# Masks carried as rows of the score products, attention moved earlier, and four more pairs by seven products, in a fused sparse-attention and bilinear-FFN kernel

## The chip, the cores and the metric

The kernel runs on one core of one Trainium2 chip. A core has a matrix engine (PE, with its weight loads shown apart as PEld), three engines for elementwise work (DVE, ACT and POOL), an engine that mostly issues transfers (SP), and 16 DMA engines. Each engine works through its own queue in order and waits on semaphores. The metric is device microseconds (us) of one execution. Three executions of the kernel before took 326.38, 330.83 and 331.78 us, a median of 330.83 us.

## The reference

Eight batches of eight heads, 576 tokens, head size 64. Heads 0 to 3 attend to the last 32 tokens, heads 4 to 7 to earlier tokens of the same residue modulo 32. The attention's output, 4608 rows of 512, goes through a bilinear FFN.

```python
scores = scale * np.matmul(q, k.transpose(0, 1, 3, 2))          # (8, 8, 576, 576)
rel = pos[:, None] - pos[None, :]
mask_local = (rel >= 0) & (rel < 32)                            # heads 0..3
mask_strided = (rel >= 0) & (pos[None, :] % 32 == pos[:, None] % 32)   # heads 4..7
scores = np.where(mask, scores, -1e9)
attn = softmax(scores)                                          # then attn @ v
x = attn_out.transpose(0, 2, 1, 3).reshape(4608, 512)
out = ((x @ w_a) * (x @ w_b)) @ w_out                           # 512 -> 1536 -> 512
```

## The kernel before, in words

**Tiles and slots.** The FFN runs over nine tiles `t` of 512 tokens. A tile has 16 slots: slots 0 to 11 make `x @ w_a` and `x @ w_b` for one block of 128 of the 1536 columns each (`ffn_ab`, block `f`), slots 12 to 15 make the output (`ffn_ys`, from tile 1 on). In a common slot PE makes eight matmuls of 512 columns into two PSUM banks, ACT copies the `w_a` bank to `a_sb` (L638), and DVE multiplies it with the `w_b` bank into `pf` (L641, L643). In tile 0 the banks come from a pool of three (`mm`); later a fourth (`tp`) joins the rotation (`mm_bank`).

**Seven products.** A pair `g` of blocks (slots 2g and 2g+1) can make its `x @ w_a` part by seven half-size products instead of eight (`a_pair_mid`, L676, in tiles 3 to 6, and `a_pair`, L736, in tiles 7 and 8). It sums into the banks X, Y and Z, copies X out several times with ACT (L714 to L731), and X's next product waits for each copy. Its inputs are differences of x quarters made by DVE (`xsum_make`, L672). `MID_A` and `FAST_A` name the pairs. The output is made in the same way: `y_plan` (L871) makes 14 groups of six matmuls of 256 columns in `Y_ORDER`, two groups for each of the products 1, 7, 6, 4, 5, 2, 3; after the second, `y_post` (L845) copies the bank with ACT (1, 7, 6, 5, 3) or adds it with DVE (4, 2).

**Attention between the slots.** Batch `b` is one of eight; its steps stand in the tables `STEPS`, `LATER` and `IN_Y` under a slot, and each is put behind that slot's work (or, at a half, between the two products of the following slot; under "y", behind that many of the 14 groups). A unit `u` is half of two heads: u = 0 to 3 are local, 4 to 7 strided. `S` makes scores into the one `st` bank pair (L381) and takes their exponent with ACT (L401), then DVE clears masked elements of `p` with a bitwise AND (`S_m`, L419). `V` multiplies by v: for local units through the `o` bank, a reciprocal and a product by DVE (L462, L470, L488); for strided units from the third batch on by `step_VT` (L510): four matmuls into `o`, four into `e` (one bank each from tile 3 on, L521), logarithms and an exponential by ACT (L533, L534), and two products by DVE (L536) that free `o` and `e`. `O` and `I` carry local outputs through DRAM to `xT`, the FFN's input.

**How q and k come.** From the third batch on, POOL issues the loads to DRAM scratch, SP issues transposing DMAs (`step_D`) into `kT_buf[b % 2]` and `qT`, and DVE copies each head of a pair to its own half of the rows of `qz_buf[b % 2]` (`step_Q`, L338); the other half is zero, so that one matmul makes the scores of both heads side by side (192 columns for local, 144 for strided units).

**POOL.** It issues the loads of q, k, v and all weights, and each issue can wait for an earlier transfer (semaphores in a ring of eight). Functions that are registered under a slot (`do(i, ...)`) stand in their engine's queue behind everything of the earlier slots. A tiny POOL copy (`pace`, L1134) holds POOL back to the work of its slot from slot 14 on; before that, nothing but its own waits does. `fill_v` (L112), under slot 0, stands behind the loads of the first two batches and of `w_a` and `w_b`, ahead of those of `w_out`.

Of the kernel before, what the change touches and what calls it, by code (L numbers as in the profile page):

```python
# [8 lines left out]
BF16 = mybir.dt.bfloat16  # L9
# [15 lines left out]
VW = 128  # L25
WCH = (0, 2, 5, 9, 12)
FAST_Y = (1, 2, 3, 4, 5, 6, 7, 8)
MID_A = {t: (1, 3) for t in (3, 4, 5, 6)}
FAST_A = {7: (1, 2, 3, 4, 5), 8: (0, 1, 2, 3, 4, 5)}
# [3 lines left out]
def kernel(  # L33
# [34 lines left out]
    def open_psum(stack, **bufs):  # L68
        for nm, n in bufs.items():
# [13 lines left out]
    kT_buf = [(const.tile([128, 2, PAD + S], BF16, name=f"kT{i}l"), const.tile([128, 2, RS * GP + 48], BF16, name=f"kT{i}s"))  # L83
              for i in range(2)]
    vl_buf = [const.tile([128, HL * 6, VW], BF16, name=f"vl{i}") for i in range(2)]
# [10 lines left out]
    def select(t, op, base, pattern, cm):  # L96
        nc.gpsimd.affine_select(out=t, in_=t, compare_op=op, fill=0.0, base=base, pattern=pattern,
                                channel_multiplier=cm)
# [1069 lines left out]
```

## Time and profile before

| | us |
|---|---|
| median of three executions | 330.83 |
| lowest, highest | 326.38, 331.78 |
| the profiled execution | 323.88 |
| its span, first to last instruction | 322.2 |
| PE busy in it | 313.8 (97%) |
| DVE busy | 248.4 (77%) |
| ACT busy | 191.4 (59%) |
| POOL busy | 120.2 (37%) |

The profile describes one execution. A line of a group gives source line, engine, operation, names out<-in, shapes and count, then the busy time of the group, the mean duration of one in ns, and the idle time of the engine before them. A line of the timeline gives the start and the duration in us, and in brackets how long the engine was idle before and who ended that. Matmuls are pipelined: the duration of one is its latency, and the distance of two starts is what it costs.

### The profile page before, as it was taken

What the parts mean: (1) busy time and instruction counts of PE and PEld (TensorE: products, weight loads), DVE (VectorE), ACT (ScalarE), POOL (GpSimd) and SP (SyncE); (2) the same over time, 40 slices, a digit from 0 to 9 for tenths busy, and PEclk for the clock granted to TensorE, in tenths of its full rate; (3) what the DMA queues carried; (4) which work ended last, traced back from release to release, by engine and by line L of the source; (5) the groups of instructions that cost most, each with busy time, mean ns of one, the idle gap of its engine ahead of it and who ended that gap; (6) DMA issues with size and microseconds to landing.
All of it is one profiled execution on the core that took longest, in us unless ns stands there. A gap on an engine that the chain in (4) does not pass through costs nothing. (4 is left out here: it accounts for less than half of the span.)

```text
span 322.2 us, 7287 instructions
## 1 busy us (share of the span) xinstructions
PE 313.8 (97%) x2738; PEld 217.9 (68%) x2766; DVE 248.4 (77%) x569; ACT 191.4 (59%) x371; POOL 120.2 (37%) x211
## 2 busy tenths in 40 slices
PE   8999999999999999999999999999999999999994
PEld 7764555455775578556999996559655866786684
DVE  6665797488867988899689868997799667857862
ACT  6763767355854476557655766577656655535541
POOL 8844850881255344315340435134001003203520
PEclk9999999999999999999999999999999999999999
DMA  8999999999599999999997999999235040004004
GB/s 154 146 203 199 203 190 209 174 146 152 119 126 144 209 148 104 144 157 172 123 120 151 164 108 131 158 203 135 18 85 121 2 127 5 0 4 130 3 0 130
DMA packets 127811, 40.41 MB, mean 125 GB/s; under 512 B 115616, under 2 KB 124896, under 8 KB 127584
## 3 DMA queue, kind: packets, MB, share of 16 engines
q0 software_dynamic: 80400, 19.28, 65.3%
q1 hardware_dynamic: 47232, 20.61, 35.9%
q8 instruction: 21, 0.34, 0.5%
q14 instruction: 14, 0.11, 0.1%
q10 hardware_dynamic: 144, 0.07, 0.1%
HBM read 39.12 MB, written 18.28 MB: 178 GB/s over the span
## 5 line engine op out<-in xcount | busy, mean ns | idle before, releaser
L617 PE MATMUL mm<-xT,wb_sb 128*128 128x512 bf16 (+1 forms) x301 | 71.6, 357 | 0.4
L617 PE MATMUL mm<-xT,wa_sb 128*128 128x512 bf16 (+1 forms) x287 | 70.2, 356 | 0.6
L638 ACT COPY a_sb<-mm 128x512 f32<-128x512 f32 x68 | 39.7, 584 | 29.5 <-PE mm L617 27.8
L1134 POOL CAST pace<-pf 1x1 f32<-1x1 bf16 x68 | 18.5, 273 | 87.6 <-DVE pf L641 41.0
L617 PEld LDWEIGHTS <-wb_sb 128*128 128x128 bf16 x312 | 30.0, 98 | 27.8 <-issue 0.7
L641 DVE TENSOR_TENSOR pf<-a_sb,mm 128x512 bf16<-128x512 f32 x58 | 39.4, 680 | 9.4 <-ACT a_sb L638 5.7
L401 ACT ACTIVATE p<-st 72x576 bf16<-72x576 f32 (+1 forms) x56 | 36.4, 650 | 15.4 <-PE st L381 14.7
L617 PEld LDWEIGHTS <-wa_sb 128*128 128x128 bf16 x312 | 27.9, 98 | 17.8
L886 PEld LDWEIGHTS <-ps 128*128 128x128 bf16 x336 | 32.6, 98 | 4.1 <-issue 0.5
L886 PE MATMUL mm<-wf,ps 128*128 128x256 bf16 x252 | 30.0, 273 | 0.3 <-ACT y_sb L851 0.3
L851 ACT COPY y_sb<-mm 128x512 f32<-128x512 f32 (+1 forms) x32 | 17.9, 558 | 19.1 <-PE mm L886 16.4
L1134 POOL COPY pace<-y_sb 1x1 f32<-1x1 f32 x21 | 8.4, 401 | 51.2 <-DVE y_sb L849 23.6
L886 PEld LDWEIGHTS <-pf 128*128 128x128 bf16 x252 | 23.6, 98 | 2.7
L766 PE MATMUL mm<-xT,wb_sb 128*128 128x512 bf16 x83 | 25.3, 379 | 0.1
L241 POOL DMA_DIRECT2D vs<-in_v_dram x24 | 21.7, 905 | 4.1 <-issue 1.7
L886 PE MATMUL mm<-wo_sb,pf 128*128 128x256 bf16 x168 | 21.8, 273 | 0.0
L820 DVE TENSOR_TENSOR ps<-pf 128x512 bf16<-128x512 bf16 (+1 forms) x49 | 19.6, 399 | 0.8
L702 PE MATMUL mm<-xT,wb_sb 128*128 128x512 bf16 (+1 forms) x80 | 19.1, 337 | 0.0
L419 DVE TENSOR_TENSOR p<-p,mask_l 128x576 int16<-128x576 int16 x32 | 14.5, 452 | 5.6 <-ACT p L401 5.5
L536 DVE TENSOR_TENSOR xT<-o,xr 64x288 bf16<-64x288 f32 x16 | 7.6, 477 | 13.5 <-ACT xr L534 13.4
L462 PEld LDWEIGHTS <-p 128*128 128x128 bf16 (+1 forms) x256 | 12.9, 97 | 7.1 <-DVE xl L488 1.1
L488 DVE TENSOR_TENSOR xl<-o,rc 96x384 bf16<-96x384 f32 x24 | 13.3, 553 | 0.8
(212 smaller groups left out, 644.0 us busy)
## 6 DMA issues: line engine op xcount, KB each, us to landing
out_dram<-y_sb SPq DMA_DIRECT2D x14, 512.0 KB, 4.6
kr<-in_k_dram POOLq DMA_DIRECT2D x12, 288.0 KB, 6.2
qr<-in_q_dram POOLq DMA_DIRECT2D x12, 288.0 KB, 7.1
vl<-in_v_dram POOLq DMA_DIRECT2D x6, 384.0 KB, 9.3
out_dram<-y_sb SPq DMA_DIRECT2D x7, 256.0 KB, 5.5
vs<-in_v_dram POOLq DMA_DIRECT2D x24, 72.0 KB, 4.9
xd<-xl SPq DMA_DIRECT2D x12, 144.0 KB, 3.3
wo_sb<-in_moe_w_out_dram POOLq DMA_DIRECT2D x4, 384.0 KB, 10.7
```

Source lines behind the costliest of these rows:

```text
L241: nc.gpsimd.dma_start(out=vs_buf[b % 2][:, h, :, 0:D], in_=v[b, HL + h].rearrange("(p r) d -> p r d", r=RS))
L401: nc.scalar.activation(p_flat(p)[:M, :2 * W].rearrange("p (i n) -> p i n", n=2 * n), st[:M].rearrange("p a (i n) -> p (a i) n", n=256)[:, ...
L419: nc.vector.tensor_tensor(pi, pi, mk, op=ALU.bitwise_and)
L617: nc.tensor.matmul(ps_[:, c0:c0 + n], lhsT=w[:, kk, 128 * f:128 * (f + 1)], rhs=xT[:, kk, x0:x0 + n], start=(kk == first and c0 == 0), sto ...
L638: nc.scalar.copy(a_sb, ab[0])
L641: nc.vector.tensor_mul(pf[:, f, :].rearrange("p (i a s) -> p a i s", i=2, s=16), halves(a_sb), halves(ab[1]))
L702: nc.tensor.matmul(dst, lhsT=wb_sb[:, kk, 128 * f:128 * (f + 1)], rhs=rhs, start=kk == 0 and k in (None, 0), stop=kk == KD - 1 and k in (N ...
L766: nc.tensor.matmul(got[e], lhsT=wb_sb[:, kk, 128 * f:128 * (f + 1)], rhs=xT[:, kk, x0:x0 + TTOK], start=kk == 0, stop=kk == KD - 1)
L820: nc.vector.tensor_tensor(s[:, n], a, b, op=op)
L851: nc.scalar.copy({"1": part(0, 0), "7": part(0, 1), "6": part(1, 0), "5": part(1, 1)}[k], bank)
L886: nc.tensor.matmul(bank[b][:, q], lhsT=lhs(g, q), rhs=rhs(g), start=k in "172" and q == 0 and g == 0, stop=g == FG - 1, skip_group_check=True)
L1134: nc.gpsimd.tensor_copy(pace, done)
```

## The change

- **Masks as rows.** From the third batch on the half of the rows that was zero carries a code of the mask, in both `kz` (two buffers for k, one per head of a pair) and `qz_buf[0]`, so that a masked element's score comes out far below zero and its exponent is 0. The AND (`S_m`) goes from there. Each head gets its own matmul: two of 96 or 72 columns in place of one of 192 or 144.
- **New copies.** `step_K` copies each head's rows from `kT_buf[0]` to `kz[j]`, two local and two strided copies of 64x1152 for each batch: by DVE, but by ACT for the local ones (K0, K1) from batch 5 on. `kz` and `qz_buf[0]` are now the same for all batches.
- **Codes.** `code_make`, on POOL behind `fill_v` under slot 0, makes four small tables by ten instructions (four MEMSETs, six selects). `fill_code` copies them into the rows: on DVE under slots 1 to 4 and 14, on ACT under slots 2, 3, 4, 5, 12 and 14 (one copy of 1152 to 1216 elements each). POOL's clearing of `qz_buf[0]` under slots 14 and 15 goes.
- **Positions.** New tables `THIRD`, `FOURTH` and `LATER`. For batches 5 to 7 S0, S1 and V0 stand within the output slots of two tiles before, the local V, O and I are earlier, V4 and V5 stand at 5.5 and 9.5; for batches 4 to 7 S7, V6 and V7 stand behind groups 1, 2 and 5 of the output (before: 2, 6 and 11), and the x differences for the next tile behind groups 7 to 10. The strided `step_D` moves from slots 10 and 11 to 8.
- **Pairs.** Tiles 4 to 6 make pairs 0, 2, 4 by seven products (before 1, 3), tile 3 pairs 2, 4, and tile 7 also pair 0. In `a_pair_mid` one matmul group of `w_b` moves ahead and pair 0 swaps two banks.

```diff
 VW = 128
+BIG = 4096.0
 WCH = (0, 2, 5, 9, 12)
 FAST_Y = (1, 2, 3, 4, 5, 6, 7, 8)
-MID_A = {t: (1, 3) for t in (3, 4, 5, 6)}
-FAST_A = {7: (1, 2, 3, 4, 5), 8: (0, 1, 2, 3, 4, 5)}
+MID_A = {3: (2, 4), 4: (0, 2, 4), 5: (0, 2, 4), 6: (0, 2, 4)}
+FAST_A = {7: (0, 1, 2, 3, 4, 5), 8: (0, 1, 2, 3, 4, 5)}
...
     qT = (const.tile([128, 2, S], BF16, name="qTl"), const.tile([128, HL * W], BF16, name="qTs"))
-    kT_buf = [(const.tile([128, 2, PAD + S], BF16, name=f"kT{i}l"), const.tile([128, 2, RS * GP + 48], BF16, name=f"kT{i}s"))
-              for i in range(2)]
-    vl_buf = [const.tile([128, HL * 6, VW], BF16, name=f"vl{i}") for i in range(2)]
+    kT_three = [(const.tile([128, 2, PAD + S], BF16, name=f"kT{i}l"), const.tile([128, 2, RS * GP + 48], BF16, name=f"kT{i}s"))
+                for i in range(3)]
+    kT_buf, kz = kT_three[::2], kT_three[1:]
+    vl_buf = [const.tile([128, HL * 6, D + 2], BF16, name=f"vl{i}") for i in range(2)]
...
         select(msl, ALU.is_ge, -1, [[-1, LW]], 1)
+    code = const.tile([32, 5, 32], BF16, name="code")
+    minus, even, odd, near = (code[:, i] for i in range(4))
+    eye = ident[:32, :32]
+    def code_make():
+        nc.gpsimd.memset(minus, -1.0)
+        nc.gpsimd.memset(even, -BIG)
+        nc.gpsimd.memset(odd, BIG)
+        nc.gpsimd.memset(near, -BIG)
+        select(minus, ALU.is_equal, 0, [[1, 32]], -1)
+        for t, op, base, step, cm, fill in ((even, ALU.is_ge, 0, 1, -1, BIG), (odd, ALU.is_ge, 0, 1, -1, -BIG),
+                                            (near, ALU.is_ge, 0, -1, 1, -4 * BIG), (near, ALU.is_ge, 1, 1, -1, -4 * BIG),
+                                            (near, ALU.is_ge, -1, 0, 1, -4 * BIG)):
+            select(t, op, base, [[step, 32]], cm, fill)
+    def kz0_zero():
+        nc.vector.memset(kT_three[1][0][:, :, :PAD], 0.0)
+        nc.vector.memset(kT_flat(kT_three[1][1])[:, HL * W:], 0.0)
+    def fill_code(nm, j, part):
+        r = 64 * (1 - j)
+        wide = lambda t, n: t.unsqueeze(1).unsqueeze(1).to_broadcast([32, 2, n, 32])
+        if part < 3:
+            t = kz[j][0] if nm == "k" else qz_buf[0][j][0]
+            t = t.rearrange("p c (g t) -> p c g t", t=32)
+            n = t.shape[2]
+            if part == 2:
+                src = (eye if nm == "k" else near)[:, :n].unsqueeze(1).unsqueeze(3).to_broadcast([32, 2, n, 32])
+                nc.scalar.copy(t[r + 32:r + 64], src)
+            else:
+                src = ((eye, minus) if nm == "k" else (even, odd))[part]
+                nc.vector.tensor_copy(t[r:r + 32, :, part::2], wide(src, (n + 1 - part) // 2))
+        elif nm == "k":
+            t = kz[j][1].rearrange("p c n -> p (c n)")[r:r + 64, :HL * W].rearrange("p (h i c) -> p h i c", h=HL, c=4)
+            nc.scalar.copy(t, nm_l[:64, :NP].unsqueeze(1).unsqueeze(3).to_broadcast(list(t.shape)))
+        else:
+            t = qz_pair[0][1][r:r + 64, j].rearrange("p c g n -> p (c g) n")
+            nc.vector.tensor_copy(t, nm_r[:64].unsqueeze(1).to_broadcast(list(t.shape)))
...
         r = slice(64 * j, 64 * j + 64)
-        dst = qz_buf[b % 2][j][z][r]
+        dst = qz_buf[0][j][z][r]
         nc.vector.tensor_copy(dst.rearrange("d c r n -> d (c r n)") if z else dst, qT[z][r])
+    def step_K(b, z, j):
+        r = slice(64 * j, 64 * j + 64)
+        part = (lambda t: kT_flat(t)[r, :HL * W]) if z else (lambda t: t[r, :, PAD:])
+        (nc.vector.tensor_copy if z or b < FIRST_D + 3 else nc.scalar.copy)(part(kz[j][z]), part(kT_buf[0][z]))
...
         kT = kT_buf[b % 2][c // 2]
         st = pst.tile([128, 2, 512], F32, tag="st", name="st")
...
                 k0 = (G * half + i) * (LW if c < 2 else GP)
-                if c < 2:
-                    rhs = qz_pair[b % 2][0][:, c % 2, :, k0:k0 + n]
-                elif b < FIRST_D:
-                    rhs = qz_pair[b % 2][1][:, :, c % 2, G * half + i]
-                if c < 2 or b < FIRST_D:
-                    lhs = kT[:, c % 2, k0:k0 + 128]
-                else:
-                    k0 = W * (u - HL) + i
-                    lhs = kT_strided(b)[:, k0:k0 + 509:4]
-                    rhs = qz_pair[b % 2][1].rearrange("p j c (e h) n -> p j (c e) h n", h=HL)[:, :, i, u - HL]
-                nc.tensor.matmul(sv[:, i, :2 * n].rearrange("p (j n) -> p j n", j=2), lhsT=lhs, rhs=rhs, start=True, stop=True)
+                if b < FIRST_D:
+                    rhs = qz_pair[1][0][:, c % 2, :, k0:k0 + n] if c < 2 else qz_pair[1][1][:, :, c % 2, G * half + i]
+                    nc.tensor.matmul(sv[:, i, :2 * n].rearrange("p (j n) -> p j n", j=2), lhsT=kT[:, c % 2, k0:k0 + 128],
+                                     rhs=rhs, start=True, stop=True)
+                    continue
+                for j in range(2):
+                    if c < 2:
+                        lhs, rhs = kz[j][0][:, c % 2, k0:k0 + 128], qz_buf[0][j][0][:, c % 2, k0:k0 + n]
+                    else:
+                        k0 = W * (u - HL) + i
+                        lhs = kT_flat(kz[j][1])[:, k0:k0 + 509:4]
+                        rhs = qz_pair[0][1][:, j].rearrange("p c (e h) n -> p (c e) h n", h=HL)[:, i, u - HL]
+                    nc.tensor.matmul(sv[:, i, j * n:(j + 1) * n], lhsT=lhs, rhs=rhs, start=True, stop=True)
             return
...
         S_px(b, u)
-        S_m(b, u)
+        if b < FIRST_D:
+            S_m(b, u)
...
                  12.6: "S1", 12.75: "L0 X2", 13: "s2 X3 V0 m2 L1 W3", 13.5: "V1 S3", 14: "V2 X0", 14.5: "V3", 15: "X1"},
-             2: {18: "Q0 Q1", 20: "S0", 20.5: "S1", 21: "V0", 21.5: "S2 Q2", 22: "V1 Q3", 22.5: "S3 O0", 23: "V2", 23.5: "S4",
+             2: {18: "K0 K1 Q0 Q1", 20: "S0", 20.5: "S1", 21: "V0 K2", 21.5: "S2 Q2", 22: "V1 K3 Q3", 22.5: "S3 O0", 23: "V2", 23.5: "S4",
                  24: "V3 I0 O1", 24.5: "S5", 25.5: "V4", 26: "S6", 26.5: "I1", 27: "V5", 27.5: "S7", 28.5: "V6", 30: "V7"}}
-    LATER = {-4: "Q0", -3: "Q1", -1: "S0", 0: "S1", 1: "V0", 2: "S2 Q2", 3: "V1 O0", 4: "S3 I0 Q3", 5: "V2", 6: "S4", 7: "V3 O1", 8: "S5", 9: "V4 I1",
-             10: "S6",
-             11: "V5"}
-    IN_Y = {2: "S7", 6: "V6", 11: "V7"}
+    THIRD = {-4: "K0 Q0", -3: "K1 Q1", -1: "S0", 0: "S1", 1: "V0 K2", 2: "S2 Q2", 3: "V1 K3 O0", 4: "S3 I0 Q3", 5: "V2", 6: "S4", 7: "V3 O1",
+             8: "S5", 9: "V4 I1", 10: "S6", 11: "V5", ("y", 2): "S7", ("y", 6): "V6", ("y", 11): "V7"}
+    REST = {4: "V3 O1 S4", 5.5: "V4", 7: "I1", 8: "S5", 9.5: "V5", 11: "S6", ("y", 1): "S7", ("y", 2): "V6", ("y", 5): "V7",
+            ("y", 7): "x0", ("y", 9): "x1 x2", ("y", 10): "x3"}
+    FOURTH = {-4: "K0 Q0", -3: "K1 Q1", -1: "S0", 0: "S1 K2", 1: "V0 S2 Q2", 2: "V1 O0 S3 K3", 3: "V2 I0 Q3", **REST}
+    LATER = {-7: "K0", -6: "K1 Q0", -5: "Q1", ("y", -6): "S0", -3: "K2", ("y", -3): "S1", ("y", -2): "V0", -2: "K3",
+             0: "S2 Q2", 1: "V1 O0", 2: "S3 Q3", 2.5: "V2", 3: "I0", **REST}
     FN = {"Tk": step_Tk, "Tq": step_Tq, "S": step_S, "V": step_V, "X": step_X, "W": lambda b, n: fast_w(n, slice(0, 3)),
           "s": S_px, "m": S_m, "L": lead_vl, "O": rows_out, "I": rows_in, "Pk": lambda b, c: pair_up("k", c), "Pq": lambda b, c: pair_up("q", c),
-          "Q": lambda b, n: step_Q(b, n // 2, n % 2)}
+          "Q": lambda b, n: step_Q(b, n // 2, n % 2), "K": lambda b, n: step_K(b, n // 2, n % 2),
+          "x": lambda b, n: xsum_make(b, n)}
...
         Y, Z, b1, b0 = [mm_bank([128, TTOK]) for _ in range(4)]
+        if g == 0:
+            Z, b1 = b1, Z
         Y, Z = Y[:, :HT], Z[:, :HT]
...
         yield p7[:1, :1]
+        b_mm(b0, 0, (0,))
         P(X, ws(0), xs(0))
         nc.scalar.copy(quarter(1, 1), X)
-        b_mm(b0, 0, (0,))
+        b_mm(b0, 0, (1,))
         P(Z, w(1, 1), xs(3))
...
         add(quarter(1, 1), p7)
-        b_mm(b0, 0, (1, 2, 3))
+        b_mm(b0, 0, (2, 3))
         P(X, ws(3), x(1, 1))
...
         do(0, fill_v, vs_buf[0])
+        do(0, code_make)
+        do(2, kz0_zero)
         for c in range(4):
...
                 do(g0 + (12 if b == FIRST_D + 1 else 7), load_vl, b)
-            gs = {2: (13, 14, 15, 15), 3: (6, 6, 14, 15)}.get(b) or (3, 4, 10, 11)
+            gs = {2: (13, 14, 15, 15), 3: (6, 6, 14, 15)}.get(b) or (3, 4, 8, 8)
             for (z, nm), g in zip(((0, "k"), (0, "q"), (1, "k"), (1, "q")), gs):
...
                 do(16 * 2 + (2, 5, 7, 9, 11, 13, 14, 15)[2 * n + c], wsum_make, n, c)
-        for t in MID_A:
-            do(16 * t - 1, xsum_make, t, 0)
-            for n in (1, 2, 3):
-                do(16 * t, xsum_make, t, n)
-        do(16 * (NT - 2) - 1, xsum_make, NT - 2, 0)
-        for n in (2, 1, 3):
-            do(16 * (NT - 2), xsum_make, NT - 2, n)
+        do(47, xsum_make, 3, 0)
+        for n in (1, 2, 3):
+            do(48, xsum_make, 3, n)
         for n in range(4):
...
         do(4, zero_qz, 1, nc.vector, ((1, 0),))
-        for i, jz in ((14, (0, 0)), (14, (1, 0)), (15, (0, 1)), (15, (1, 1))):
-            do(i, zero_qz, 0, nc.gpsimd, (jz,))
+        do(1, fill_code, "q", 0, 3)
+        do(1, fill_code, "q", 1, 3)
+        for i, j in ((2, 0), (3, 1)):
+            for part in (2, 0, 1):
+                do(i, fill_code, "q", j, part)
+        do(4, fill_code, "k", 0, 3)
+        for part in (0, 1):
+            do(4, fill_code, "k", 0, part)
+        do(5, fill_code, "k", 0, 2)
+        do(12, fill_code, "k", 1, 3)
+        for part in (2, 0, 1):
+            do(14, fill_code, "k", 1, part)
         do(2, fill_v, vs_buf[1])
```

More of the change, by code (lines that the diff above doesn't have):

```diff
@@ L94, with select @@
     msl = const.tile([128, LW], F32, name="msl")
-    def select(t, op, base, pattern, cm):
-        nc.gpsimd.affine_select(out=t, in_=t, compare_op=op, fill=0.0, base=base, pattern=pattern,
+    def select(t, op, base, pattern, cm, fill=0.0):
+        nc.gpsimd.affine_select(out=t, in_=t, compare_op=op, fill=fill, base=base, pattern=pattern,
                                 channel_multiplier=cm)
@@ L314, in T_e, with kT_flat @@
                     perm(qz_buf[b % 2][j][c // 2][pr, c % 2]), tv[pr])
-    def kT_strided(b):
-        return kT_buf[b % 2][1].rearrange("p c n -> p (c n)")
+    def kT_flat(t):
+        return t.rearrange("p c n -> p (c n)")
     def step_D(b, z, nm):
@@ L324, in step_D @@
         if z == 0:
-            nc.sync.dma_start(out=kT_buf[b % 2][0][:, :, PAD:] if nm == "k" else qT[0],
+            nc.sync.dma_start(out=kT_buf[0][0][:, :, PAD:] if nm == "k" else qT[0],
                               in_=rows.rearrange("t h d -> t (h d)"), transpose=True)
         elif nm == "k":
-            nc.sync.dma_start(out=kT_strided(b)[:, :HL * W], in_=rows.rearrange("h (t e) d -> (h t) (e d)", e=2), transpose=True)
+            nc.sync.dma_start(out=kT_flat(kT_buf[0][1])[:, :HL * W], in_=rows.rearrange("h (t e) d -> (h t) (e d)", e=2), transpose=True)
         else:
@@ L1056 @@
         for b in range(1, B):
-            for pos, names in (STEPS.get(b) or {16 * (b - 1) + x: n for x, n in LATER.items()}).items():
+            for pos, names in (STEPS.get(b) or (THIRD if b == 3 else FOURTH if b == 4 else LATER)).items():
+                if isinstance(pos, tuple):
+                    pos = ("y", b - 1, pos[1]) if pos[1] > 0 else ("y", b - 2, 14 + pos[1])
+                elif b not in STEPS:
+                    pos += 16 * (b - 1)
                 steps.setdefault(pos, []).append((b, names.split()))
-            if b not in STEPS:
-                for n, names in IN_Y.items():
-                    steps["y", b - 1, n] = [(b, names.split())]
         at = {}
```

## The prediction

> **What bounds the kernel now.** I read the engines' shares first, then the groups with shapes kept apart, then the timelines around the waits that the change makes or moves. The first line of the page:
>
> ```profile
> PE 313.8 (97%) x2738; PEld 217.9 (68%) x2766; DVE 248.4 (77%) x569; ACT 191.4 (59%) x371; POOL 120.2 (37%) x211
> ```
>
> PE is busy throughout; from 22 us on the chain of waits hardly leaves it. So a time is won only by fewer columns on PE, and lost whenever an engine makes PE wait. Groups of PE (mean duration of one behind the comma):
>
> ```profile
> L617 PE MATMUL mm<-xT,wb_sb 128*128 128x512 bf16 x237 | 62.9, 379 | 0.4
> ...
> L462 PE MATMUL o<-vl,p 128*128 128x65 bf16 x192 | 11.0, 194 | 0.8 <-DMA vl<-in_v_dram 0.5 <-DVE xl L488 0.3
> ...
> L521 PE MATMUL o<-p,vs 72*128 72x72 bf16 x128 | 8.1, 196 | 0.0
> L381 PE MATMUL st<-qz1s,kT1s 128*128 128x144 bf16 x64 | 6.6, 226 | 0.0
> L381 PE MATMUL st<-qz1l,kT1l 128*128 128x192 bf16 x48 | 6.6, 246 | 0.0
> ```
>
> These durations are latencies. In the timeline four 72-column products together take 0.29, so one costs (0.29 - 0.196) / 3 = 0.03 us; in the same way 96 columns cost 0.043 (the transposes), 144 0.061, 192 0.082, 256 0.109, 512 0.216.
>
> Next POOL's timeline, where the new tables will be made:
>
> ```profile
> 22.21 0.68 POOL L236 DMA_DIRECT2D tk<-in_v_dram  x1 [2.72 <-PE ab L617]
> ...
> 28.77 0.76 POOL L250 DMA_DIRECT2D wb_sb<-in_moe_w_b_dram  x1 [1.98 <-DMA wb_sb<-in_moe_w_b_dram]
> ...
> 31.78 1.80 POOL L112 MEMSET vs<- 72x2016 bf16 x1
> 33.50 3.02 POOL L253 DMA_DIRECT2D wo_sb<-in_moe_w_out_dram  x4
> ```
>
> The MEMSET is `fill_v`, registered under slot 0, which PE leaves at about 22.4. POOL is 9 us late because its issues wait for earlier transfers (8.1 us of idle in this stretch). ACT at that time is at slot 2:
>
> ```profile
> 23.98 0.58 ACT L638 COPY a_sb<-mm 128x512 f32<-128x512 f32 x1 [0.32 <-PE mm L617]
> 25.66 0.59 ACT L638 COPY a_sb<-mm 128x512 f32<-128x512 f32 x1 [1.10 <-PE mm L617]
> ```
>
> Last, an output phase (groups of 12 matmuls), where V6 and V7 move closer:
>
> ```profile
> 220.97 0.29 PE L521 MATMUL o<-p,vs 72*128 72x72 bf16 x4
> ...
> 221.22 0.58 ACT L851 COPY y_sb<-mm 128x512 f32<-128x512 f32 x1 [0.77 <-PE mm L886]
> ...
> 221.83 0.43 ACT L533 ACTIVATE xr<-o 64x288 f32<-64x288 f32 x1
> ...
> 222.60 0.68 ACT L534 ACTIVATE xr<-xr 64x576 f32<-64x576 f32 x1
> 223.32 0.47 DVE L536 TENSOR_TENSOR xT<-o,xr 64x288 bf16<-64x288 f32 x1 [2.02 <-ACT xr L534]
> 223.70 0.46 DVE L536 TENSOR_TENSOR xT<-e,xr 64x288 bf16<-64x288 f32 x1
> ...
> 224.51 0.30 PE L521 MATMUL o<-p,vs 72*128 72x72 bf16 x4
> ```
>
> V6 begins at 220.97, behind group 6; `o` is free 2.82 us later, `e` 3.19 us later; V7 begins 3.54 us later, behind group 11. It has 0.7 us to spare.
>
> **The parts.**
>
> *Columns.* A local unit goes from 3 x 0.082 = 0.246 to 6 x 0.043 = 0.258, a strided one from 4 x 0.061 = 0.244 to 8 x 0.033 = 0.264: with 48 units +0.6 to +0.8 us. Four more pairs go from 8 x 0.216 = 1.73 to 14 x 0.109 = 1.53: -0.8. Net about **-0.2**. No row shows weights taken with a step of four for 72 columns; those weight loads last 113 ns against 98 in a row, so the price of 192 of them lies between 0 and 192 x 0.015 = +2.9. I take 0, since 72-column products with fresh weights run at 0.03 (L521).
>
> *The wait for the tables.* In the changed kernel's order ACT has, right behind slot 2's copy (23.98 to 24.57), the copy of `near`, which waits for POOL's last select. POOL makes the tables behind `fill_v`: 33.6 plus four MEMSETs of some 0.11 and six selects of 0.28 to 0.36 (rows of L97) gives 36.0. Then ACT takes 1.15 for its copy of 1152 elements (row L122: 64x1152, 1149 ns) and 0.58 for slot 3's `a_sb`: 37.7. Behind the waiting ACT stand all later `a_sb` copies. DVE waits too, behind slot 2's multiply. With three banks PE gets through slot 3 and the first half of slot 4; slot 4's `w_b` matmuls need slot 3's `w_a` bank, which ACT has not copied. They began at 27.19. PE has nothing else in its queue: **37.7 - 27.2 = +10.5** (9 to 11.5, as the transfers land). Nothing wins it back, since PE is full afterwards. POOL's `w_out` loads go 2.4 us later, but before PE needs them; ACT's other code copies lie in its idle time (in slots 2 to 5 a copy of 0.58 each 1.73; under slots 12 and 14 idle stretches of 0.6 and 2.1).
>
> *The clock after it.* At the start of the span 23 matmuls of 224 columns take 4.45 us, 0.185 each; later ones 0.1. So after being idle PE runs at half pace until 5.9 us, 5.0 us after its first. If 10 us of idle do the same, half of 5.0 is lost: **+2.5** (0 to 2.5; the row of the start is the nearest). [...]
>
> *S6 and S7, tiles 3 to 6.* They are now one group, 0.66, apart. Both use the one `st` bank, and S7 needs S6's exponent done: 0.2 after the products to its start, 0.65, and 0.05 back to PE, so 0.24 late even with ACT free, as in tile 6. In tiles 3 to 5 ACT isn't free. K0 and K1, 1.15 each (L122 again), now stand on ACT behind slots 9 and 10. Counted from slot 8's start, ACT has five pair copies of 0.37, S5's exponent 0.65, K0 1.15, V5's 0.43 + 0.42 + 0.68, `a_sb` 0.58, K1 1.15, `a_sb` 0.58, S6's exponent 0.65: 8.1 us, plus 1.6 of waits for the pair's first products, less 0.6 of overlap of neighbours: it ends at 9.1. PE reaches S7 behind group 1 after 1.74 + 0.27 + 1.52 + 2.0 + 2.0 + 0.66 = 8.2, where the bank is free at 9.1: 0.95 late each. With tile 6 **+3.1** (1.0, if ACT has no backlog, to 4.5).
>
> *V6 and V7, tiles 3 to 6.* Now three groups apart: V6's 0.27 plus 3 x 0.656 = 2.24 us, where `o` needs 2.82 and then `e` 3.19, with the same bank copy ahead of V6 on ACT. V7 waits 0.6, then 0.25 more: 0.85 each, **+3.4** (0 to 4).
>
> *Others.* Pair 0 of tile 7 at its head copies X behind the output's last copy, as tile 8 does now (289.60 to 289.98 ahead of a matmul at 290.03, 0.24 late): +0.25. 48 ANDs of 0.45 leave DVE, 24 K copies (18 on DVE) of 0.45 to 0.5 and three pairs' sums of 0.41 come: it is 77% busy, so only V1's wait at 76 us (0.3, for L488) may go: **-0.3**. The one set of `kz` and `qz_buf[0]` is refilled only behind its last reader: K0 stands seven slots behind S3, K2 six groups behind S7. On SP the strided transposes move ahead of nothing that PE is late for: kT landed 5 to 7 us after issue, K2 stands five slots (11 us) behind. V0's `vl` landed about 9 us after issue, and V0 comes some 13 us after; that cover is 4 us.
>
> Sum: -0.2 + 10.5 + 2.5 + 3.1 + 3.4 + 0.25 - 0.3 = **+19.2**. On the profiled execution's own 323.88 us (span 322.2) that is 343.1. That execution was faster than the three timed ones; their median is 330.83. On the mean of all four, 328.2, it gives **347**, which I predict.
>
> **The rivals.**
>
> *The wait alone* (0.20): tables late, but ACT and DVE overlap so well that the output phases don't stall, or the clock holds: +10 to +13, 338 to 341. For it: PE stalled nowhere in those phases before.
>
> *The tables in time* (0.10), not slower by over 2%: if POOL has the tables by 25.4 (27.2 less ACT's 1.15 and 0.58), the wait costs nothing, and the rest, +6, gives 334; with no stall in the output 328. Even without its 8.1 us of idle POOL would end at 27.9, 2.5 too late. Against it: 31.78 in the view of POOL.
>
> *Attention sooner pays* (0.03): the timed executions are 2.5 to 7.9 us above the profiled one; if that is PE waiting for late `xT` at tile heads, earlier V7 wins it back, about -5, for 324. It decides only if the tables are in time. The trace shows no such wait.
>
> *Weight loads in a row* (0.05): were each split product held by its own load, 144 at 0.098 and 192 at 0.113 would replace 12.0 us by 35.8: +24 alone, and some 370 with the rest. Against it: 65 and 72 columns at 0.03 with a fresh load each. [...]
>
> **How the numbers follow.** Forecast 0.62, the wait alone 0.20, tables in time 0.10, attention sooner 0.03, loads in a row 0.05. The range reaches from the wait alone on the lower base to the forecast's terms at their upper ends, 337 to 354; it holds the first two cases, 0.82. 2% of 330.83, about what a measurement can tell from no change, is 6.6 us: faster 0.02, within 0.11, slower 0.87.
>
> **What the profile after would show.** PE idle from about 27 to 37, with ACT's first code copy waiting for POOL; 512-column matmuls 0.43 apart for some us behind it; S7 waiting for ACT and V7 for DVE in tiles 3 to 6; no AND after the second batch; 96-column products 0.043 apart. I am wrong if POOL gets to the tables before 27 us, or if PE has other work there.

## The result, and the profile after

The changed kernel takes 345.89 us (median of four executions, 344.19 to 348.01); the kernel before, beside it, 328.61 (323.86 to 331.78). The ratio is **1.0642, with a 95% interval of 1.0495 to 1.079**: slower. The ratio compares means and leaves out executions more than 1.5% above the fastest of their kernel, here 330.83 and 331.78 us of the kernel before, while the medians are of all. The profiled execution took 344.34 us with a span of 342.6, against 323.88 and 322.2 before, so 20.4 us of span have to be found.

From the page of the changed kernel, busy time and the busy tenths of 40 slices (8.6 us each):

```profile
PE 319.8 (93%) x2950; PEld 219.7 (64%) x2950; DVE 249.4 (73%) x562; ACT 207.1 (60%) x395; POOL 117.8 (34%) x210
...
PE   8991799999999999999899989998999999999995
...
PEclk9998799999999999999999999999999999999999
```

PE is no longer full: its share falls from 97% to 93%, and the hole is one slice, the fourth (25.7 to 34.3 us), with the start of the fifth; the granted clock (PEclk) is lower in these two. The timeline of the changed kernel there (start and duration in us, in brackets the idle time before and who ended it):

```profile
26.15 1.02 PE L672 MATMUL mm<-xT,wa_sb 128*128 128x512 bf16 x4
...
31.03 1.80 POOL L114 MEMSET vs<- 72x2016 bf16 x1
...
33.00 1.32 POOL L99 TENSOR_SCALAR_AFFINE_SELECT code<-code 32x32 bf16<-32x32 bf16 x6
...
34.36 1.15 ACT L165 COPY qz0l<-code 32x1152 bf16<-32x1152 bf16 x1 [10.20 <-POOL code L99]
...
35.53 0.58 ACT L693 COPY a_sb<-mm 128x512 f32<-128x512 f32 x1
...
36.17 1.87 PE L672 MATMUL mm<-xT,wb_sb 128*128 128x512 bf16 x4 [8.99 <-ACT a_sb L693]
...
37.83 1.71 PE L672 MATMUL mm<-xT,wa_sb 128*128 128x512 bf16 x4
...
39.37 1.03 PE L672 MATMUL mm<-xT,wb_sb 128*128 128x512 bf16 x4
39.44 2.62 DVE L168 COPY kT1l<-ident 32x640 bf16<-32x640 bf16 x1
...
39.76 2.16 POOL L255 DMA_DIRECT2D qr<-in_q_dram  x1
...
43.42 0.42 PE L337 MATMUL tp<-ident,shared 72*128 72x72 bf16 x8 [1.03 <-DVE kT2s L348]
```

Read the chain downwards. POOL clears `vs`, then makes the tables; ACT has waited 10.20 us for the last select, copies `near`, and only then slot 3's `a_sb`; PE starts again 0.06 us behind that copy's end. The last four products ahead of the wait would have ended at 26.15 + 4 x 0.216 = 27.0, so 9.2 us are lost. The next eight products take 39.37 - 36.17 = 3.20 us where they cost 1.73 at full pace: 1.5 us more. In the trace the granted clock is 0.50 from 32.4 to 39.2 us and 1.00 on both sides. The last lines are a loss that I had not forecast: DVE's copy of `ident`, 0.30 us for the second buffer at 67 us, took 2.62, and PE waited for DVE.

The output phase of tile 4, timeline of the changed kernel:

```profile
197.94 1.15 ACT L387 COPY kT2l<-kT0l 64x1152 bf16<-64x1152 bf16 x1
...
199.12 0.58 ACT L693 COPY a_sb<-mm 128x512 f32<-128x512 f32 x1
...
199.60 0.65 ACT L451 ACTIVATE p<-st 72x576 bf16<-72x576 f32 x1
...
200.30 0.19 PE L431 MATMUL st<-qz0s,kT1s 128*128 128x72 bf16 x1 [1.04 <-ACT p L451]
...
201.22 0.29 PE L572 MATMUL o<-p,vs 72*128 72x72 bf16 x4
...
203.55 0.48 DVE L587 TENSOR_TENSOR xT<-o,xr 64x288 bf16<-64x288 f32 x1 [1.48 <-ACT xr L585]
...
204.08 0.29 PE L572 MATMUL o<-p,vs 72*128 72x72 bf16 x4 [0.47 <-DVE xT L587]
```

K1 (L387) stands on ACT ahead of `a_sb` and S6's exponent, and S7 waits for that exponent; V7 waits for V6's product that frees `o`. Both steps are the ones forecast.

The 20.4 us, each term read as PE's time beyond what its columns need, the same stall of the kernel before taken off:

| | forecast | measured, us |
|---|---|---|
| columns (split products, pairs) | -0.2 | -0.35 |
| wait for the tables | +10.5 | +9.2 |
| half pace after it | +2.5 | +1.5 |
| S7 waits for ACT, tiles 3 to 6 | +3.1 | 0.68 + 1.20 + 1.20 + 0.24 = +3.3 |
| group 1 of the output waits for `pf`, tiles 3 to 5 | none | 0.77 + 0.20 + 0.24 = +1.2 |
| V7 waits for `o` and `e`, four tiles | +3.4 | 4 x (0.63 + 0.25) = +3.5 |
| head of tile 7 | +0.25 | +0.24 |
| V1 and V2 of batch 2 wait for DVE | -0.3 | 0.80 + 0.43 - 0.44 before = +0.8 |
| tile 0 waits for DVE | none | 1.19 - 0.78 before = +0.4 |
| tile 0, slot 12 on: a transpose waits for ACT behind a code copy | none | +0.3 |
| head of tile 3 waits for `xT` | none | +0.35 |
| sum | +19.2 | +20.4 |

The first row is worked out from counts and prices; the others are read from the timeline. Two small differences in tile 0 are not in the table and partly cancel: the product that waits for the first batch's `xT` starts 0.4 us sooner than in the kernel before (21.61 against 22.01), and one at 26.15 starts 0.24 late. The columns are as the groups of the prediction gave them, with weights taken in steps of four too: in the changed kernel's timeline eight 72-column products start 0.033 apart and 96-column ones 0.043.

### The profile page after: what moved, and what is told of

It reads as the page before. It is cut to its first block, busy times and chain, and to the rows that moved or that the text cites. A ratio compares the mean times of both kernels' runs of the same rounds, so it can differ in the third digit from the quotient of the medians.

```text
span 342.6 us, 7683 instructions
## 1 busy us (share of the span) xinstructions
PE 319.8 (93%) x2950; PEld 219.7 (64%) x2950; DVE 249.4 (73%) x562; ACT 207.1 (60%) x395; POOL 117.8 (34%) x210
## 4 chain that ended last, share of the span: by engine, by line
PE 64%; ACT 10%; DMA 7%; POOL 5%; SPq 5%; DVE 4%; issue 4%; POOLq 0%; ACTq 0%; DVEq 0%
PE mm L672 19%; PE mm L944 12%; PE mm L824 6%; PE mm L759 6%; DMA wb_sb<-in_moe_w_b_dram 4%; PE ax L817 3%; PE st L431 3%; PE e L745 3%; PE mm L817 2%; PE mm L1006 2%; PE mm L745 2%; SPq L374 2%; ACT p L451 2%; DMA xd<-xl 2%; POOL shared L246 2%
## 5 line engine op out<-in xcount | busy, mean ns | idle before, releaser
L672 PE MATMUL mm<-xT,wa_sb 128*128 128x512 bf16 (+1 forms) x264 | 63.1, 363 | 0.3 <-DMA xT<-xd 0.2
L672 PEld LDWEIGHTS <-wb_sb 128*128 128x128 bf16 x272 | 25.3, 98 | 32.9 <-issue 11.0
L693 ACT COPY a_sb<-mm 128x512 f32<-128x512 f32 x60 | 34.6, 585 | 17.3 <-PE mm L672 16.9
L696 DVE TENSOR_TENSOR pf<-a_sb,mm 128x512 bf16<-128x512 f32 x50 | 34.0, 680 | 11.5 <-ACT a_sb L693 6.4
L672 PEld LDWEIGHTS <-wa_sb 128*128 128x128 bf16 x272 | 24.5, 98 | 18.4 <-issue 1.5
L824 PE MATMUL mm<-xT,wb_sb 128*128 128x512 bf16 x96 | 28.5, 379 | 0.0
L1201 POOL COPY pace<-y_sb 1x1 f32<-1x1 f32 x17 | 5.3, 313 | 55.3 <-DVE y_sb L907 25.3
L284 POOL DMA_DIRECT2D vs<-in_v_dram x24 | 22.7, 949 | 4.6 <-issue 2.7
L944 PE MATMUL mm<-wo_sb,pf 128*128 128x256 bf16 x168 | 22.7, 273 | 0.7 <-DVE pf L696 0.6
L587 DVE TENSOR_TENSOR xT<-o,xr 64x288 bf16<-64x288 f32 x16 | 7.6, 478 | 16.6 <-ACT xr L585 16.6
L767 DVE TENSOR_TENSOR a_sb<-mm,a_sb 128x256 f32<-128x256 f32 x22 | 9.3, 422 | 7.5 <-ACT a_sb L782 5.6
L764 DVE TENSOR_TENSOR pf<-a_sb,mm 128x512 bf16<-128x512 f32 x22 | 14.1, 683 | 0.4
```

Source lines behind the costliest of these rows:

```text
L284: nc.gpsimd.dma_start(out=vs_buf[b % 2][:, h, :, 0:D], in_=v[b, HL + h].rearrange("(p r) d -> p r d", r=RS))
L672: nc.tensor.matmul(ps_[:, c0:c0 + n], lhsT=w[:, kk, 128 * f:128 * (f + 1)], rhs=xT[:, kk, x0:x0 + n], start=(kk == first and c0 == 0), sto ...
L693: nc.scalar.copy(a_sb, ab[0])
L696: nc.vector.tensor_mul(pf[:, f, :].rearrange("p (i a s) -> p a i s", i=2, s=16), halves(a_sb), halves(ab[1]))
L824: nc.tensor.matmul(got[e], lhsT=wb_sb[:, kk, 128 * f:128 * (f + 1)], rhs=xT[:, kk, x0:x0 + TTOK], start=kk == 0, stop=kk == KD - 1)
L944: nc.tensor.matmul(bank[b][:, q], lhsT=lhs(g, q), rhs=rhs(g), start=k in "172" and q == 0 and g == 0, stop=g == FG - 1, skip_group_check=True)
```

## The experiments

In the comparisons that follow the kernel before stood at 323.2 to 323.3 us (median). Where no interval is given, a kernel was executed once; such a run is read by the waits in its trace, since executions of one kernel differ by some us. "Tables early" below is the changed kernel with `code_make` at its earlier place.

### The tables early

```diff
                     load_w(2)
+                    code_make()
                     load_qk(1, True, (0, 1))
...
-        do(0, code_make)
```

> The changed kernel with the four tables made by POOL ahead of its blocked loads (behind the third pair of w_a and w_b loads) in place of behind fill_v. Theory (the late tables hold ACT, ACT holds PE, then the clock): PE's 9.4 us of waiting at 27 to 36 us and the half pace behind it (1.5 us) go, the span falls from 342.6 to about 331.5, and the ratio to the kernel before is near 1.03; the waits of S7 and V7 in tiles 3 to 6 stay as they are. Rival (the loads themselves are what PE would wait for next): another wait of PE of some us shows in tile 0 and the span stays above 336.

Measured: 333.42 us, **1.0308 (1.0265 to 1.0351)** of the kernel before; span 331.3, 11.3 less than the changed kernel. Timeline of this kernel:

```profile
15.40 1.24 POOL L99 TENSOR_SCALAR_AFFINE_SELECT code<-code 32x32 bf16<-32x32 bf16 x6
...
24.49 1.15 ACT L165 COPY qz0l<-code 32x1152 bf16<-32x1152 bf16 x1
...
27.16 1.03 PE L672 MATMUL mm<-xT,wb_sb 128*128 128x512 bf16 x4
```

The tables are ready at 16.6, 8 us before ACT wants them, the `w_b` products of slot 4 start at 27.16, and neither the wait nor the half pace is left. So more than half of the loss is the place of ten POOL instructions. The waits of the output phases stand unchanged, and tile 3's head waits 0.71 us.

### The wait alone

The kernel before, with the tables made behind `fill_v` and one copy of `near` by ACT behind slot 2 (`fill_spot`, 32x1152 into the zero rows of `qz_buf[0]`, which are cleared again later), and nothing else of the change.

```diff
         do(0, fill_v, vs_buf[0])
+        do(0, code_make)
+        do(2, fill_spot)
```

> The kernel before with nothing but the tables on POOL behind fill_v under slot 0 and one copy of the table near by ACT behind slot 2 (into rows that are cleared later; output unchanged). Theory: this alone costs about 9.4 us of waiting and 1.5 us at half pace: span 322.2 to about 333, ratio about 1.033. Rival (the split products and the new schedule are what costs): under 325, ratio within 1.01.

Measured: 334.93 us, **1.035 (1.0305 to 1.0394)**; span 333.1, 10.9 over before. Timeline of PE and ACT:

```profile
34.75 1.15 ACT L149 COPY qz0l<-code 32x1152 bf16<-32x1152 bf16 x1 [10.58 <-POOL code L97]
...
36.56 1.87 PE L635 MATMUL mm<-xT,wb_sb 128*128 128x512 bf16 x4 [9.49 <-ACT a_sb L656]
38.21 1.91 PE L635 MATMUL mm<-xT,wa_sb 128*128 128x512 bf16 x4
39.92 1.88 PE L635 MATMUL mm<-xT,wb_sb 128*128 128x512 bf16 x4
41.63 1.04 PE L635 MATMUL mm<-xT,wa_sb 128*128 128x512 bf16 x4
```

One copy that waits, put into a kernel in which nothing else is changed, makes the same hole. Here twelve products run at half pace, 5.07 us from 36.56 to 41.63, which cost 2.6 at full pace: 2.5 us more. That is the price I had taken, where the changed kernel paid 1.5. The half pace after nine to ten idle microseconds lasted 3.0 us of PE's work in one execution and 5.1 in another; the last section sets the stretches of low clock beside that. The wait is 9.65 us here (36.56 less 26.91, where the last product ahead of it would have ended), so wait and half pace come to 12.1. Two differences that the edit did not aim at give 1.2 back: the product that waits for the first batch's `xT` starts 0.4 us sooner (21.62 against 22.01), and the kernel before's wait of 0.76 for `tq` at 42 us does not occur.

### Busy while it waits

The changed kernel, with 84 matmuls of 224 columns (nothing reads them) ahead of slot 4's `w_b` products.

```diff
-    STEPS = {1: {5.5: "Tk2", 6: "Tq2", 7: "S4 Tk3", 7.5: "S5", 8: "Tq3", 8.5: "V4", 9: "S6 V5 Pk0", 9.5: "S7 Pq0",
+    STEPS = {1: {3.5: "H0", 5.5: "Tk2", 6: "Tq2", 7: "S4 Tk3", 7.5: "S5", 8: "Tq3", 8.5: "V4", 9: "S6 V5 Pk0", 9.5: "S7 Pq0",
...
+    def keep_warm(b, n):
+        ones = lambda n: nc.const_aps.tensor(1.0, [128, n], BF16)
+        bank = pst.tile([128, 2, 512], F32, tag="st", name="warm")
+        for _ in range(84):
+            nc.tensor.matmul(bank[:, 0, :224], lhsT=ones(128), rhs=ones(224), start=True, stop=True)
```

> The changed kernel, with 84 more matmuls of 224 columns into the st bank placed on PE ahead of slot 4's w_b products, where PE now stands idle for 9.4 us. They compute nothing that is used. Theory (PE runs at half pace because it was idle): the wait for ACT's copy of the table near stays, slot 4's w_b products still start near 36.2 us, but all that follows runs at the full pace of 0.216 us for 512 columns, so the profiled time is some 1.5 us below that of the changed kernel, 344.3: about 342.8. Rival (the first products behind the wait are slow for another reason, their operands or the copies beside them): the eight products still take 0.41 each, and the time stays at 344.3.

```profile
27.66 8.47 PE L642 MATMUL warm<-const-bfloat16-1.0 128*128 128x224 bf16 x84
36.95 1.02 PE L678 MATMUL mm<-xT,wb_sb 128*128 128x512 bf16 x3 [0.82 <-ACT a_sb L699]
37.82 1.03 PE L678 MATMUL mm<-xT,wa_sb 128*128 128x512 bf16 x4
...
44.20 0.42 PE L337 MATMUL tp<-ident,shared 72*128 72x72 bf16 x8 [2.45 <-DVE kT2s L348]
```

In PE's timeline the first products behind the wait are 0.216 apart, and the granted clock stays at 1.00, where it was 0.50 in the changed kernel. They had been slow because PE had been idle, and for no reason of their own. The time went the other way, to 350.09 us: in this execution POOL had the tables 0.8 us later, PE waited 2.45 us for DVE at 44.2 (1.03 in the changed kernel), and further on there were waits that other executions don't have. So the theory on the clock holds in the trace, while the time that I gave with it was missed: waits elsewhere are larger than the 1.5 us looked for. (The four executions of the changed kernel lie 3.8 us apart, too; whether by such waits isn't shown, as only one has a profile.)

### The copies of k on DVE

```diff
-        (nc.vector.tensor_copy if z or b < FIRST_D + 3 else nc.scalar.copy)(part(kz[j][z]), part(kT_buf[0][z]))
+        nc.vector.tensor_copy(part(kz[j][z]), part(kT_buf[0][z]))
```

(with the tables early)

> As tables_early, with K0 and K1 of batches 5 to 7 by DVE in place of ACT. Theory (ACT's backlog ahead of the output makes S7 late): in tiles 3 to 5 S7's wait falls from 0.7 to 1.2 us to 0.24, as in tile 6, and the small waits on pf in groups 1 and 2 go with it: 3 to 4 us less than tables_early. Rival (DVE has no room for 6 x 0.45): waits on DVE of the same size appear (V, pf or the x differences) and the span stays within 1 us of tables_early.

Measured: 330.13 us, span 328.4, 2.9 less than with the tables early alone. S7 no longer waits in tile 3, and in tiles 4, 5 and 6 it waits 0.24 each, the part that I had worked out as left with ACT free. Group 1's waits for `pf` fall from 1.2 to 0.3 (tile 3). V7 stands where it was, at 4 x 0.89:

```profile
191.10 0.29 PE L572 MATMUL o<-p,vs 72*128 72x72 bf16 x4 [0.47 <-DVE xT L587]
```

The gain of 3.5 is partly given back: the head of tile 3 waits 1.48 us for `xT`, 0.77 more than with the tables early.

### V7 later

```diff
-    REST = {4: "V3 O1 S4", 5.5: "V4", 7: "I1", 8: "S5", 9.5: "V5", 11: "S6", ("y", 1): "S7", ("y", 2): "V6", ("y", 5): "V7",
-            ("y", 7): "x0", ("y", 9): "x1 x2", ("y", 10): "x3"}
+    REST = {4: "V3 O1 S4", 5.5: "V4", 7: "I1", 8: "S5", 9.5: "V5", 11: "S6", ("y", 1): "S7", ("y", 2): "V6", ("y", 7): "V7",
+            ("y", 8): "x0", ("y", 11): "x1 x2", ("y", 12): "x3"}
```

(with the tables early)

> As tables_early, with V7 of batches 4 to 7 behind group 7 of the output in place of 5, and the x differences behind 8, 11, 11 and 12. Theory (the o and e banks are free only 2.8 and 3.2 us after V6 began): V7's waits of 0.63 + 0.25 in four tiles go, 3.5 us less than tables_early. Rival (the time is only moved): PE waits at the heads of tiles 4 to 7 for the x differences or for e, and less than 1 us is won.

Measured: 333.39 us, as much as without the edit. The cause is confirmed all the same: of the attention's steps in an output phase only S7 still waits (group 1's waits for `pf` stay), and V7 at 196.38 starts behind group 7 with no idle time ahead of it:

```profile
191.84 0.19 PE L431 MATMUL st<-qz0s,kT1s 128*128 128x72 bf16 x1 [1.04 <-ACT p L451]
...
196.38 0.29 PE L572 MATMUL o<-p,vs 72*128 72x72 bf16 x4
```

The 3.5 us that this gains were lost in the same execution to waits for DVE at 33.5 us (1.77), at 41.9 us (1.46) and for `xT` at the head of tile 3 (0.38 more). None of these places is touched by the edit, and the first two don't appear with the tables early. Something in tile 0 was different from one execution to the next, and it was DVE's copies: the code copy that took 0.43 us with the tables early took 2.60 here, from 29.80. POOL began to issue the load of `shared` 0.04 us ahead of it and then cleared `vs` (MEMSET, to 32.23); the copy ended 0.17 us behind that. With the tables early the same issue began 0.40 us behind the copy's start. The next runs follow that.

### The order on SP

```diff
-            gs = {2: (13, 14, 15, 15), 3: (6, 6, 14, 15)}.get(b) or (3, 4, 8, 8)
+            gs = {2: (13, 14, 15, 15), 3: (6, 6, 14, 15), 4: (3, 4, 10, 11)}.get(b) or (3, 4, 8, 8)
```

(with the tables early)

> Tables early, and for batch 4 alone the strided step_D goes back to slots 10 and 11, behind batch 3's I1 (slot 9) on SP. Theory (I1's transpose stands on SP behind the five strided transposes and so reaches xT late): the wait for xT at the head of tile 3, 0.71 us with tables early (0.35 in the changed kernel, 1.09 and 1.48 in the two other runs with tables early), goes; all other waits stay; 330.0 to 332.8 against 333.4. Rival (the transfer itself is slow, or its DRAM write is late): the wait stays.

SP's timeline in the changed kernel, and then in this one (L371 and L374 are batch 4's strided transposes, L559 is the transpose of batch 3's I1):

```profile
125.08 4.24 SPq L371 DMA_TRANSPOSE kT0s<-kr  x1
129.37 7.02 SPq L374 DMA_TRANSPOSE qTs<-qr  x4
136.49 1.21 SPq L559 DMA_TRANSPOSE xT<-xd  x1
```

```profile
119.94 1.16 SPq L559 DMA_TRANSPOSE xT<-xd  x1
121.15 1.88 SPq L371 DMA_TRANSPOSE kT0s<-kr  x1
```

Measured: 332.56 us; the wait at the head of tile 3 is gone, and all else stays, but for 0.31 us at 133.3, where V waits for DVE, behind a K2 copy that took 0.90 us beside an issue of POOL. So the strided transposes had been moved past the one transpose that tile 3's head is waiting for, which still stood in slot 9 for batch 3.

### DVE's copies beside POOL's issues

First K2 of batch 2 moved half a slot up, with the tables early:

```diff
-             2: {18: "K0 K1 Q0 Q1", 20: "S0", 20.5: "S1", 21: "V0 K2", 21.5: "S2 Q2", 22: "V1 K3 Q3", 22.5: "S3 O0", 23: "V2", 23.5: "S4",
+             2: {18: "K0 K1 Q0 Q1", 20: "S0", 20.5: "S1 K2", 21: "V0", 21.5: "S2 Q2", 22: "V1 K3 Q3", 22.5: "S3 O0", 23: "V2", 23.5: "S4",
```

> Tables early, and K2 of batch 2 stands at 20.5 in place of 21. With tables early V1 and V2 of that batch wait 0.80 and 0.43 us for DVE's xl, behind a K2 copy that took 1.17 us beside a POOL that issues loads of v. Theory (a DVE copy lengthens only while POOL is at work beside it, and DVE is short of time just there): sooner, the copy takes 0.45 to 0.6 unless POOL's issue of kr, at 68.1 to 69.7, lies beside it, the two waits come to 0.5 us at most, and the time is 0.7 lower. Rival (the copy is slow because it is the first of its form or reads a fresh transpose): 1.17 again, waits hardly smaller.

Timelines of DVE and POOL with the tables early, and then in this kernel, with PE:

```profile
69.17 2.21 POOL L255 DMA_DIRECT2D qr<-in_q_dram  x1
...
70.48 1.17 DVE L387 COPY kT1s<-kT0s 64x1152 bf16<-64x1152 bf16 x1
```

```profile
68.66 1.68 POOL L255 DMA_DIRECT2D kr<-in_k_dram  x1
...
69.01 3.25 DVE L387 COPY kT1s<-kT0s 64x1152 bf16<-64x1152 bf16 x1
...
69.77 2.21 POOL L255 DMA_DIRECT2D qr<-in_q_dram  x1
...
73.61 0.36 PE L513 MATMUL o<-vl,p 128*128 128x65 bf16 x6 [1.98 <-DVE xl L539]
```

Measured: 336.46 us, 3 us worse where 0.7 less was forecast, and more telling than a gain (0.76 of the 3 us is a wait for `tq` in tile 0, which the edit doesn't touch). The copy, 1.17 us at its old place and 0.44 where POOL is quiet, took 3.25 here. It started while POOL issued `kr` and ended 0.3 us behind the end of the issue of `qr` (71.98). The condition that I had written down (unless POOL's issue lies beside it) came true in full. PE waited 2.15 us for it, and six of its next eight 512-column products ran at half pace.

Then POOL moved and DVE left alone, with the tables early:

```diff
-                    do((16, 18, 19, 20)[h], load_vs, b, (h,))
+                    do((16, 18, 19, 19)[h], load_vs, b, (h,))
...
-                do(19 if b == FIRST_D + 1 else g0 - 2, load_qk, b, False)
+                do(16 if b == FIRST_D + 1 else g0 - 2, load_qk, b, False)
```

> Tables early; DVE's work and every step of the attention stay where they are, but POOL issues batch 3's local loads of k and q under slot 16 in place of 19, and batch 2's last load of v under 19 in place of 20, so that POOL issues nothing while K2 of batch 2 is copied. Theory (what lengthens the copy is POOL's issuing beside it): K2's copy takes 0.45 us in place of 1.17, and V1's wait of 0.80 falls by about that, to 0.1 or less, V2's 0.43 to 0.2 or less, some 0.9 in all; the copies of 64x1152 that now lie beside POOL's moved issues become the long ones. Rival (the copy is long because it is the first strided one after a fresh transpose): 1.17 again, and the waits stay.

Timelines of DVE and POOL in this kernel:

```profile
63.84 2.19 POOL L255 DMA_DIRECT2D qr<-in_q_dram  x1
...
64.22 2.09 DVE L387 COPY kT1l<-kT0l 64x1152 bf16<-64x1152 bf16 x1
...
71.99 0.44 DVE L387 COPY kT1s<-kT0s 64x1152 bf16<-64x1152 bf16 x1
```

Measured: 334.44 us. K2's copy is down from 1.17 to 0.44 and V1's wait of 0.80 is gone (V2's stays at 0.40). The whole is slower, as K0's copy, 0.45 before, now lies beside the moved issue and takes 2.09, S0 waits 0.69 and 0.45 us for DVE, and in this execution a `tq` copy in tile 0 cost 0.76 and the head of tile 3 1.45. The slow copy follows POOL's issues; the rival, a copy slow by its form or its source, is out.

### All repairs together

Tables early, k copied by DVE, S6 at 10.5, V7 behind group 8 with the differences behind 9, 11 and 12, batch 4's `step_D` behind I1, three code copies from slots 4 and 12 to 15, and K2 of batch 2 at 20.5.

> Every wait found is met by a change of place and nothing else: tables made right behind the load of w_a and w_b blocks 0 to 2; DVE makes all copies of k; S6 at 10.5; V7 behind group 8 with the x differences behind groups 9, 11 and 12; batch 4's strided step_D back behind I1; K2 of batch 2 at 20.5; two code copies of DVE and one of ACT moved from slots 4 and 12 to 15. Masks as rows, split products, the four more pairs and the early local outputs stay. Theory (the loss is the sum of the waits listed, and the columns are worth 0.35 us): span 331.3 less 0.30, 0.7, 0.7, S7's 3.3 and V7's 3.5 gives about 322.8, that is the time of the kernel before to within 0.5%: ratio 0.997 to 1.006. Rival (the masks as rows or the early attention cost something that the waits do not show, or one repair makes a new wait of the same size): ratio over 1.01.

Measured: 328.30 us, **1.0143 (1.0117 to 1.0168)**, which is the rival's range (over 1.01) and its second case: in the output phases only 0.32 us (tile 3) and 0.34 (tile 6) are left, but a repair had made a new wait, K2's copy of 3.25 us again, with 2.15 us of waiting and 1.2 of half pace behind it. So K2 and K3 of batch 2 went to ACT, with K2 back at 21:

```diff
-        nc.vector.tensor_copy(part(kz[j][z]), part(kT_buf[0][z]))
+        (nc.scalar.copy if z and b == FIRST_D else nc.vector.tensor_copy)(part(kz[j][z]), part(kT_buf[0][z]))
```

> As the kernel repaired, except that K2 of batch 2 is back at 21 and ACT, not DVE, makes K2 and K3 of that batch. In repaired PE stood idle for 2.15 us at 73 us behind a K2 copy of 3.2 us on DVE, and ran at half pace for about 3.4 us after that, 1.4 us more. Theory (an ACT copy isn't lengthened by POOL's issuing, and those two losses are all that lies between repaired and the kernel before, but for 1 us of smaller waits): 3.5 us less than repaired, about 324.8, ratio to before 1.001 to 1.008. Rival (the DVE copy is only moved on, or ACT becomes late for the exponents of S2 and S3): over 326.5, ratio over 1.010.

From the page of this kernel:

```profile
PE 316.2 (98%) x2950; PEld 219.7 (68%) x2950; DVE 248.3 (77%) x566; ACT 202.2 (63%) x391; POOL 119.9 (37%) x210
```

Measured: 325.24 us, **1.007 (1.0039 to 1.01)**; the profiled execution took 323.99 with a span of 322.3, where the kernel before had 323.88 and 322.2. ACT's copy of `kT1s` took 1.15 us beside POOL's issue of `qr`, as the ACT copies of this size did in the changed kernel (1.15). In that profile PE's waits come to 0.4 us more than in the kernel before, and the columns give 0.35 back. That profiled execution is one of the two fastest of twelve, though, and the interval stays above 1: with the waits found removed, masks as rows, the early attention and four more pairs together win nothing and, by that interval, still cost 0.4 to 1.0%. Nearly all of the 20.4 us were waits and half pace; what the last 0.7% is, no profile shows.

## Why the prediction was right or wrong

The forecast was 347 us in a range of 337 to 354, slower at 0.87; 345.89 was measured. On the profiled execution it was 343.1, with 344.34 measured. The sum held because its four large steps were right, and because errors of both signs cancelled, which is luck: 2.3 us too much for the wait and the clock, 3.4 us that I had not forecast.

- **Wait for the tables** (+10.5 forecast, 9.2 measured). The mechanism was right step by step, and the wait alone in the kernel before makes it again (9.65). The size was 1.3 too large, mainly since the tables came at 34.3 and not at 36.0: `fill_v` ended 0.8 sooner (32.8, not 33.6), and the ten POOL instructions took 1.6 us, not 2.4. Six selects in a row cost 1.32, not 6 x 0.3, and the four MEMSETs, 0.14 to 0.15 each, began 0.06 apart and so lay over each other.
- **Half pace** (+2.5 forecast, 1.5 and in the other kernel 2.5 measured). Cause shown by the busy PE. The size was taken from a single case, the start of the span, while the length of the slow stretch differs from run to run.
- **S6 and S7** (+3.1, 3.3 measured, with K1 on ACT as the cause shown by the run without it). The 0.95 for each of three tiles was 0.68, 1.20 and 1.20. Missed was that the same late ACT also makes DVE's last `pf` late, for which the output's first group waits: 1.2 more.
- **V6 and V7** (+3.4, 3.5 measured): 0.63 + 0.25 against 0.6 + 0.25, in all four tiles, and gone when V7 stands two groups later.
- **V1 in tile 1** (-0.3 forecast, +0.8 measured). This step failed. I argued from DVE's share of 77% and from the ANDs that leave it. But V1 is reached before they do any good: K2 is a new copy just there, POOL issues beside it, and it takes 1.17 us.
- **SP** ("ahead of nothing that PE is late for"). Wrong for one batch. I checked the landing of what was moved and not what it was moved past: batch 3 still followed the old positions (I1 in slot 9), while batch 4's transposes followed the new ones (slot 8). The price was 0.35 us here and 0.7 to 1.5 with the tables early.
- **Columns, head of tile 7**: as forecast, weights with a step of four at the lower end of their range. The heads of tiles 5 and 6, 0.24 us each as in tile 7, show only once the tables are early.
- **The base.** I put the sum on 328.2, the mean of four executions, as the three timed ones were 2.5 to 7.9 us above the profiled one. In all later comparisons the median of before was 323.2. On the two shorter of the four (mean 325.1) the sum would have given 344.3, and on 323.2 it would have given 342.4; that 347 lies 1.1 us from 345.89 is in part luck. Why the first four spread so far isn't settled.

Of the rivals, the wait alone made 11 of 20 us, and the output phases did stall; the tables in time would have given 334 (333.42 measured with the tables moved); attention sooner shows no gain in any run; loads in a row did not occur (72-column products 0.033 apart).

What stays open: executions of the last kernel range from 323.82 to 329.84 us, and only one of 323.99 has a profile. That tile 0's copies meet POOL's issues in some executions and not in others would explain it. Two traces show such a pair (tables early and V7 later: one copy, 0.43 and 2.60 us), but for the executions of the last kernel it is only argued.

## What to carry to other kernels

A step that is registered under a slot is only as early as the engine that feeds it: look in the trace for when that engine really gets there, and who in which queue stands behind the waiting instruction, since one copy that waited for 10.2 us on ACT cost PE 9.2. When steps are moved up, compare for each queue the last step that keeps its old place with the first that has the new one, and leave between two uses of a bank the whole round trip that the profile shows (here 2.8 us for `o` and 3.2 for `e`). And don't let a copy on DVE start while POOL issues DMAs (0.44 us became up to 3.25 here); ACT, dearer by the copy (1.15 against 0.45), kept its duration.

## What the runs showed of the hardware that was not expected

**A DVE copy can be held up by POOL's issue of a DMA.** A copy of 64x1152 bf16 takes 0.44 us on DVE with POOL quiet. Beside POOL's issues it took 1.17, 2.09 and 3.25, the last over two issues in a row; a 32x640 copy took 0.30 and 2.62. DVE's products into `pf`, one input of which lies in PSUM, kept their 0.66 to 0.69 us beside the same issues, and ACT's copies of 64x1152 their 1.15. To lie beside an issue is not enough. The twelve profiles hold 504 DVE copies of 64x1152. None of the 349 that started outside an issue took over 0.48 us, and beside 79 of these an issue began later. Of the 155 that started within an issue, 62 took over 0.5 us, and each of them ended 0.25 to 0.31 us behind the end of an issue; 93 kept their time, and 76 of these had started in the issue's first 0.3 us. What decides for the rest is open. A long MEMSET on POOL holds such copies up too (in the run with V7 later the 2.60 us, and 0.77 for a `tq` copy that takes 0.34; they ended about 0.2 us behind a MEMSET).

What holds such a copy until POOL's issue or MEMSET has ended, no run here shows. In the kernel before one such copy cost 0.76 us at 42 us (`tq`, 1.10 us for a copy that takes 0.34), which the prediction had not seen.

**Short idling can cost the clock too.** In the two runs with K2 sooner PE was idle for 2.0 us, and the granted clock then fell to 0.50 for 3.4 us: from 74.2 to 77.7 with K2 alone moved, 0.6 us after PE had started again, and from 73.9 to 77.3 in the kernel with all repairs. After 2.45 us in the run with the busy PE it did not fall, while in the same run after waits of 1.0, 1.1 and 0.6 us within 3.5 us it did (172.8 to 176.2). So how long PE has to be idle for it, no run here shows. The clock is at 0.50 for 3.4 us in these three cases, for 6.8 in the changed kernel (32.4 to 39.2) and for 10.2 with the wait alone (31.4 to 41.7), about once, twice and three times the 3.4; what sets these lengths is open. The half pace cost 1.5 us in one kernel and 2.5 in the other since PE started again at different distances from the end of the slow stretch: 3.0 us ahead of it in the first (36.17), 5.1 us in the other (36.56).
